# Casting weight transfers, fp32 sums, a spare accumulator bank and a rank table in an attention-and-mixer kernel

## The chip, the cores and the metric

The kernel runs on one core of a Trainium2 chip. The metric is the device time of one execution in microseconds (us); lower is better. The kernel before takes 185.1 us (median of 3 runs, 184.88 to 185.16). Each profiled run also has a span (first to last recorded instruction) and a granted TensorE clock, 1.0 being full speed; within one run the span is about 1.75 us shorter than the time (185.26 and 183.5 in the profiled run before). A "half clock" is 0.5.

## The reference

Four batches, each an attention part (a gated recurrence, 8 heads of 48) and a mixer with two pairs of products. Cut to what matters:

```python
# attention, per batch and head; q, k, v, f_logit: (4, 8, 768, 48) fp32
f = 1 / (1 + exp(-f_logit))
for t in range(768):
    state = f[t][:, None] * state + outer(k[t], v[t])
    y[t] = q[t] @ state
# mixer, per batch; x: (768, 384), the heads side by side
h  = relu(x.T @ w_tok1) @ w_tok2        # w_tok1 768x256, w_tok2 256x768
u  = x + h.T
out = u + relu(u @ w_ch1) @ w_ch2       # w_ch1 384x1536, w_ch2 1536x384
```

The kernel does the recurrence in chunks of 128 steps, two at a time (a "pair"; three pairs a batch). It needs running sums of log f within a chunk, the exponentials of their positive and negative, gated q and k, scores under a mask, and a state that is carried on.

## The kernel before

The kernel describes its work as 972 operations (960 after the change), each with the engines that may do it, an estimated duration and a priority. A planner in the file simulates the engines and emits the instructions in the order that it finds. So a change of a duration, a priority or a part moves instructions everywhere. `patience` is 0 in this kernel. The parts that matter here:

```python
# which ready operation goes next: earliest start, then priority
key = (round(st + self.patience * max(o.prio, -20.0), 2), o.prio, st + occ)
...
# running sums: Ln = ln(1 + exp(-f)); two rows are added (Pf), split into
# a bf16 high part and the bf16 rest, and summed by two bf16 matmuls
P.op(f"hi{i}", {"POOL": ..., "ACT": ...}, [f"Pf{i}"], [f"hi{i}"], ...)    # cast
P.op(f"lo{i}", flex, [f"hi{i}", f"Pf{i}"], [f"L{i}"], ...)                # Pf - hi
nc.tensor.matmul(s3, lhsT=tri2, rhs=hi[:, :, 0:D], start=True, stop=False)
nc.tensor.matmul(s3, lhsT=tri2, rhs=lo[:, :, 0:D], start=False, stop=False)
...
# token weights: fp32 loads after the last v of batch 0, then casts
P.op("w1l", {"SP": (0.7, 0)}, [], ["w1s"], <load>, -400, [tail])
P.op(f"w1c{j},{kk}", {"POOL": ..., "ACT": ...}, ["w1s"], [f"w1{kk}"], <cast>)
# first channel weights: casting DMAs that start after a gate
gates = dict(zip(("wc1a", "wc1b", "wc2a", "wc2b"), ("w2s1", "-", "q1,1", "-")))
...
# products that nobody uses, in TensorE's planned gaps, to keep its clock up
FILL = (1.6, 60.0)        # us of the plan in which they may stand
```

"First token product" below is x times w_tok1, "second token product" is times w_tok2, "channel products" are times w_ch1 and w_ch2, "unused products" are those of the last lines.

## Time and profile before

The profile's own lines are in the prediction further down. This is what they come to; "channel stretch" is from the start of the first channel product to the end of the last, the "ramp" is what comes before it and the "tail" what comes after. A matmul's recorded time overlaps that of the next one (326 ns each, 162.5 ns apart), so a TensorE that reads as busy can still lose time.

| before | us | where it is read |
|---|---|---|
| time, span | 185.1, 183.5 | runs, page |
| end of batch 0's first token product | 35.1 | chain of waits |
| first channel product | 41.0 | chain of waits |
| channel stretch | 137.9 | chain of waits |
| last addition and stores | 4.6 | chain of waits |
| TensorE idle in the channel stretch | 3.4 | windows, below |

In a row of windows the columns are: the stretch, its length, then busy time (and count) of PE (TensorE), PEld (its weight loads), DVE (VectorE), ACT (ScalarE) and POOL (GpSimd), then the clock, the DMA share and GB/s.

### The profile page before, as it was taken

What the parts mean: (1) busy time and instruction counts of PE and PEld (TensorE: products, weight loads), DVE (VectorE), ACT (ScalarE), POOL (GpSimd) and SP (SyncE); (2) the same over time, 40 slices, a digit from 0 to 9 for tenths busy, and PEclk for the clock granted to TensorE, in tenths of its full rate; (3) what the DMA queues carried; (4) which work ended last, traced back from release to release, by engine and by line L of the source; (5) the groups of instructions that cost most, each with busy time, mean ns of one, the idle gap of its engine ahead of it and who ended that gap; (6) DMA issues with size and microseconds to landing.
All of it is one profiled execution on the core that took longest, in us unless ns stands there. A gap on an engine that the chain in (4) does not pass through costs nothing.

```text
span 183.5 us, 5042 instructions
## 1 busy us (share of the span) xinstructions
PE 170.7 (93%) x2050; PEld 105.9 (58%) x2050; DVE 121.7 (66%) x232; ACT 119.6 (65%) x215; POOL 67.9 (37%) x114
## 2 busy tenths in 40 slices
PE   6899979999999999999989999789999999999990
PEld 2346655576666766565656666266666656666550
DVE  7489865698857688998499996998944166012021
ACT  2879689999767688767777935369338542924800
POOL 3017882365374337386543935365210100000000
PEclk9999997999999999999999999999999999999999
DMA  6999999989993999999999999991352011303033
GB/s 151 261 261 263 298 326 241 209 206 257 203 209 85 279 257 264 187 187 214 222 268 189 201 274 136 201 240 25 46 84 73 0 45 45 86 0 88 4 91 81
DMA packets 69159, 31.00 MB, mean 169 GB/s; under 512 B 63120, under 2 KB 68496, under 8 KB 69136
## 3 DMA queue, kind: packets, MB, share of 16 engines
q1 hardware_dynamic: 66768, 28.32, 72.7%
q0 software_dynamic: 2368, 2.36, 7.8%
q8 instruction: 16, 0.26, 0.6%
q14 instruction: 7, 0.06, 0.1%
HBM read 25.17 MB, written 4.72 MB: 163 GB/s over the span
## 4 chain that ended last, share of the span: by engine, by line
PE 58%; DVE 15%; DMA 10%; ACT 9%; issue 4%; POOL 1%; DVEq 0%; ACTq 0%; POOLq 0%
PE pp L902 21%; PE pp L927 18%; DMA v_ld<-in_v_dram 8%; DVE qkh L618 3%; DVE xu L861 3%; PE pp L839 2%; ACT G L577 2%; DMA f_ld<-in_f_logit_dram 2%; PE pp L876 2%; DVE AmT L733 2%; PE pp L855 2%; ACT xu L823 2%; PE pp L641 2%; PE pp L798 2%; PE pp L983 2%
## 5 line engine op out<-in xcount | busy, mean ns | idle before, releaser
L927 PE MATMUL pp<-w_ch,zT 128*128 128x384 bf16 x288 | 52.2, 326 | 0.0
L902 PE MATMUL pp<-uT,w_ch 128*128 128x384 bf16 x288 | 51.5, 326 | 0.6 <-DVE zT L911 0.4
L909 ACT ACTIVATE zT<-pp 128x384 bf16<-128x384 f32 x72 | 34.9, 491 | 18.1 <-PE pp L902 17.9
L902 PEld LDWEIGHTS <-w_ch 128*128 128x128 bf16 x288 | 26.9, 98 | 17.2 <-issue 1.0
L927 PEld LDWEIGHTS <-zT 128*128 128x128 bf16 x288 | 27.0, 98 | 16.5 <-issue 0.2
L937 DVE TENSOR_TENSOR xu<-xu,pp 128x384 f32<-128x384 f32 x24 | 13.2, 551 | 29.2 <-PE pp L927 29.0
L983 PE MATMUL pp<-idle 128*128 128x512 bf16 (+4 forms) x82 | 20.7, 339 | 1.5 <-DVE idle L379 1.5
L481 POOL CAST v_bf<-v_ld 64x384 bf16<-64x384 f32 (+1 forms) x28 | 16.2, 577 | 15.8 <-DMA v_ld<-in_v_dram 14.7
L776 DVE TENSOR_TENSOR AmT<-pp,msk 128x1024 bf16<-128x1024 f32 x12 | 14.4, 1219 | 3.0 <-PE pp L769 3.0
L481 POOL CAST x_bf<-xu 128x768 bf16<-128x768 f32 x10 | 8.2, 824 | 20.9 <-ACT xu L823 20.8
L911 DVE TENSOR_SCALAR zT<-pp 128x384 bf16<-128x384 f32 x24 | 12.7, 554 | 4.6 <-PE pp L902 3.7
L733 DVE TENSOR_TENSOR AmT<-pp,msk 128x1024 bf16<-128x1024 f32 x12 | 14.1, 1217 | 2.4 <-PE pp L725 2.3
L607 POOL TENSOR_TENSOR qkh<-q_ld,G 128x384 bf16<-128x384 f32 x14 | 13.0, 940 | 2.4 <-ACT glast L574 2.3
L618 DVE TENSOR_TENSOR qkh<-k_ld,pp 64x384 bf16<-64x384 f32 x24 | 13.2, 550 | 0.5
L983 PEld LDWEIGHTS <-idle 128*128 128x128 bf16 x82 | 7.9, 104 | 8.3 <-issue 2.8
L861 DVE TENSOR_TENSOR xu<-xu,pp 128x384 f32<-128x384 f32 x24 | 11.7, 547 | 0.1
L548 POOL TENSOR_TENSOR Plo<-Pf,Phi 128x384 bf16<-128x384 f32 x10 | 9.1, 914 | 7.0 <-ACT Phi L479 4.5
L536 ACT ACTIVATE f_ld<-f_ld 128x768 f32<-128x768 f32 x12 | 10.1, 838 | 2.5 <-DMA f_ld<-in_f_logit_dram 2.5
L577 ACT ACTIVATE G<-pp 128x768 bf16<-128x768 f32 x12 | 9.7, 811 | 2.8 <-DVE pp L566 2.0
L823 ACT COPY xu<-pp 128x768 f32<-128x768 f32 x11 | 8.8, 797 | 4.1 <-PE pp L786 2.0
L479 ACT CAST u_bf<-xu 128x768 bf16<-128x768 f32 x8 | 6.5, 831 | 6.9 <-DVE xu L861 6.7
L855 PE MATMUL pp<-h1T,w_tok 128*128 128x384 bf16 x48 | 9.9, 325 | 1.3 <-DVE xu L937 1.1
(99 smaller groups left out, 249.4 us busy)
## 6 DMA issues: line engine op xcount, KB each, us to landing
f_ld<-in_f_logit_dram SPq DMA_DIRECT2D x12, 384.0 KB, 5.1
q_ld<-in_q_dram SPq DMA_DIRECT2D x12, 384.0 KB, 6.2
k_ld<-in_k_dram SPq DMA_DIRECT2D x12, 384.0 KB, 6.0
v_ld<-in_v_dram SPq DMA_DIRECT2D x12, 384.0 KB, 6.5
out_dram<-xu SPq DMA_DIRECT2D x22, 192.0 KB, 2.9
w_ch<-in_moe_w_ch_dram POOLq DMA_DIRECT2D x4, 576.0 KB, 9.4
w1s<-in_moe_w_tok_dram SPq DMA_DIRECT2D x1, 768.0 KB, 7.6
v_ld<-in_moe_w_tok_dram SPq DMA_DIRECT2D x1, 384.0 KB, 6.0
```

The source lines that it names most:

```text
L481: (nc.vector if e == "DVE" else nc.gpsimd).tensor_copy(o, x)
L577: P.op(f"G{i}", {"ACT": act_t(768)}, [f"S{i}", f"S1{i}"], [f"G{i}"], lambda: nc.scalar.activation(P[f"G{i}"].rearrange("t j h d -> t j (h ...
L618: nc.vector.tensor_tensor(o, x, g, ALU.mult)
L733: lambda e=e: nc.vector.tensor_tensor(P[f"Am{e}{i}"], P[f"A{e}{i}"].rearrange("p b (a t) -> p (b a) t", t=128), msk2.rearrange("p j t -> p ...
L776: lambda j=j: nc.vector.tensor_tensor(P[f"Am{j}{i}"], P[f"A{j}{i}"].rearrange("p b (a t) -> p (b a) t", t=128), msk[:, j].rearrange("p j t ...
L855: nc.tensor.matmul(pm[:, 0:DM], lhsT=w_tok2[:, kt, tt * 128:(tt + 1) * 128], rhs=P[f"h1{b}"][:, kt, :], start=(kt == 0), stop=(kt == 1))
L861: nc.vector.tensor_tensor(x, x, P[f"up{i}"][:, 0:DM], ALU.add)
L902: nc.tensor.matmul(pm, lhsT=w_ch1[:, kt, cc * 128:(cc + 1) * 128], rhs=uT[:, 3 * th:3 * th + 3, kt, :], start=(kt == 0), stop=(kt == 2))
L909: nc.scalar.activation(P[f"z{i}"], P[f"zp{i}"][:, 0:384], AF.Relu)
L927: nc.tensor.matmul(P[f"op{i}"][:, 0:DM], lhsT=P[f"z{b},{th},{cc}"][:, c0:c0 + 128], rhs=w_ch2[:, cc, :], start=(cc == 0), stop=(cc == NCC ...
L937: nc.vector.tensor_tensor(x, x, P[f"op{i}"][:, 0:DM], ALU.add)
L983: nc.tensor.matmul(P.psum_tile[:, bank, 0:n], lhsT=idle[:, 0:128], rhs=idle[:, 0:n], start=True, stop=True)
```

## The change

Its intent: take casts and subtractions away from the engines that bound the start, let the token weights arrive without an engine's help, and replace the formula for priorities by a table of ranks that was searched for by replaying traces (so the record says; the diff holds only the table). The core of the diff:

```diff
+RANKS = """ 563 564 565 ... 374 """            # one rank per operation, cut
-key = (round(st + self.patience * max(o.prio, -20.0), 2), o.prio, st + occ)
+key = (int(st * 100.0 + 0.5), o.prio, st + occ)
+for o, rank in zip(P.ops, RANKS.split()):
+    o.prio = int(rank)
 # durations corrected, e.g.
-P.op(f"av{i},{e}", {"PE": (0.165, PE_LAT)}, ...
+P.op(f"av{i},{e}", {"PE": (0.205, PE_LAT)}, ...
 # 1. token weights: three casting DMAs from GpSimd, gated on a landed v load
+gates = ... ("w10","w11"), ("w2",), ("wc1a","wc1b","wc2a","wc2b")
+            -> ("v0,1", "-", "-", "q1,0", "-", "q1,2", "-")
 # 2. the bf16 high part read in place
+return P[f"Pf{i}"].bitcast(BF16).rearrange("p h (d two) -> p h d two", two=2)[:, :, :, 1]
 # 3. batch 0, pairs 1 and 2: sums by fp32 matmuls
+nc.tensor.matmul(hd(P[f"S{i}"][:, a, 0:DM]), lhsT=tri2f[:, 0], rhs=x[:, :, 0:D], ...)
 # 4. second token product in two 64-column halves, so that w_tok2 needs no reordering
+w = w_tok2[:, kt, tt * 128:(tt + 1) * 128].rearrange("r (p two) -> r two p", two=2)
+for j in range(2):
+    nc.tensor.matmul(pm[64 * j:64 * j + 64, 0:DM], lhsT=w[:, j], rhs=P[f"h1{b}"][:, kt, :], ...)
 # 5. last output tile in two halves of 192 columns, its two stores on two queues
 # 6. one PSUM bank (accumulator memory) kept free for unused products until 30 us of the plan, before 26
-    P.spare = 26.0
+    P.spare = 30.0
```

## The prediction

> **What bounds the kernel now.** I read the page's busy shares and slices first, then the chain of waits in order of time, then a table by stage, then the groups by shape for what one instruction costs.
>
> ```profile
> span 183.5 us, 5042 instructions
> PE 170.7 (93%) x2050; PEld 105.9 (58%) x2050; DVE 121.7 (66%) x232; ACT 119.6 (65%) x215; POOL 67.9 (37%) x114
> PE   6899979999999999999989999789999999999990
> PEclk9999997999999999999999999999999999999999
> ```
>
> TensorE looks full, but 20.7 us of its 170.7 are products that nobody uses (82 matmuls of the tile `idle` that keep its clock up), and a matmul is counted with its drain, so 93% hides small gaps. So I did not use busy time. I took start-to-start times: 36 matmuls of 384 columns take 5.85 us in the chain, 0.1625 us each, while the group's mean of one is 326 ns.
>
> ```profile
> 14.97 7.02 DMA v_ld<-in_v_dram
> 22.01 0.76 ACT v_bf L479
> 22.77 0.79 ACT xu L823
> ...
> 27.37 0.80 ACT xu L823
> 28.20 0.84 ACT w_tok L479
> 29.17 0.58 PE pp L839 x2
> ...
> 33.08 1.35 PE pp L983 x7
> 34.43 0.65 PE pp L839 x4
> ...
> 41.02 1.08 PE pp L902 x6
> ...
> 104.20 7.53 DMA v_ld<-in_v_dram
> ...
> 118.43 1.94 DVE xu L861 x4
> ...
> 173.05 5.86 PE pp L927 x36
> 178.93 0.55 DVE xu L937
> ```
>
> The reader should see three parts. Until 41.0 us there is a ramp: batch 0's attention waits for loads (the last v load lands at 22.0), then for ScalarE (casts, evictions, and a token-weight cast at 28.2), and only at 41.02 does the first channel matmul (L902) start. From there to 178.9 the chain is mostly TensorE, with one excursion through a v load and VectorE that ends at 123. Then 4.6 us of tail: one addition and the stores.
>
> ```profile
> 23.00:41.00 18.00, 16.13 (x257) 10.96 (x257) 12.53 (x22) 16.41 (x27) 10.01 (x15) 0.91 1.07 244
> 112.00:124.00 12.00, 9.94 (x116) 5.74 (x114) 10.61 (x18) 6.28 (x11) 6.81 (x13) 1.00 1.00 204
> 124.00:179.00 55.00, 54.90 (x465) 33.72 (x463) 22.10 (x40) 28.23 (x56) 5.12 (x8) 1.00 0.22 49
> 30.00:31.00 1.00, 1.00 (x23) 0.94 (x18) 0.23 (x1) 1.00 (x3) 0.00 (x0) 0.50 1.20 232
> ```
>
> The columns are PE, PEld, DVE, ACT, POOL busy, clock, DMA share, GB/s. In the ramp's second half ScalarE is the full engine (16.4 of 18 us). In 112 to 124 VectorE is (10.6 of 12), and TensorE starves. After 124 TensorE is dense and nothing can be won but the tail. At 30 us the clock was granted at half.
>
> **What the Trainium skill says.** (1) "TensorE: Matmul & The Clock Gate", Part 1: an idle window of about 3.4 us halves the clock. The trace agrees in size: the clock falls after the 0.8 us hole in TensorE at 26.2 and stays 0.5 for about 3.4 us (0.71, 0.50, 0.50, 0.58 in the slices from 29 to 33). It also says warm spacing is N/2.4 GHz plus 2.5 ns, 162.5 ns at 384; measured 162.5. (2) "FP8 and Floating Point Precision", TensorE Precision Notes: true FP32 takes four passes. No fp32 matmul runs in the kernel before; the estimate is 4 x 0.1625 = 0.65 us for 384 columns. (3) "DMA: Bandwidth & Descriptors", SWDGE vs HWDGE: a casting transfer must come from GpSimd's software queue; the section on queues adds that engines take the queues in turn. The trace agrees as far as it goes: the four casting transfers of w_ch cost GpSimd 0.86 us each to issue and land after 7.7 to 12.3 us. (4) "TensorEngine Tiling (Array Packing)", Key Properties: changing the tiling mode drains TensorE. Nothing in the trace before isolates that.
>
> **The change part by part.**
> 1. *Token weights by casting DMA.* Removed: casts of w_tok, ScalarE 2 x 0.83 + 0.52 = 2.2 us, GpSimd 2 x 0.83 = 1.7, VectorE 3 x 0.55 = 1.6, all between 24.3 and 31.0, where ScalarE is full. Added: three software DMAs, 3 x 0.86 = 2.6 us of GpSimd, behind one more gate copy (0.19). They start when v of pair 1 has landed (about 16 us) and run beside the last q, k, v loads. The bytes read are the same 1.57 MB, and the DMA engines are at 260 GB/s, so what they take from v of pair 2 is up to 3 us, but the token weights then land beside it and not after it.
> 2. *High half as a view.* The bf16 high part is read in place from the fp32 sum: 12 casts go (ScalarE 8 x 0.51 = 4.1 us, GpSimd 4 x 0.57 = 2.3). In the ramp two of them lie in the chain itself (0.40 and 0.52 at 6.95 and 8.72).
> 3. *fp32 sums in batch 0, pairs 1 and 2.* Removed: two low-part subtractions (0.56 on VectorE, 0.91 on GpSimd) and two S0 subtractions (2 x 0.56). Added on TensorE: 3 fp32 matmuls of 384 columns and 4 tiny ones per pair, 3 x 0.65 + about 0.5 = 2.45 against 0.53 us, so +3.8 us in all, put where TensorE otherwise runs unused products.
> 4. *Second token product in two 64-column halves.* 48 matmuls become 96; if the two halves run side by side the time is the same 7.8 us; the instruction order has five unbroken groups, perhaps 0.2 us of drain each: +1.
> 5. *Last tile in halves, its store on two queues.* The addition falls from 0.55 to about 0.29, and one store issue (0.6) no longer stands behind another: tail 4.6 to 3.8 us.
> 6. *Order and spare bank.* The built orders differ on all engines. Before the first channel matmul the changed TensorE order holds 27,136 columns of unused products, as many as before, but all token products of batch 0 (24 of the second, in one block, against 12) and batch 1's first pair up to its scores.
>
> **The sum.** Counting matmuls in each built order and multiplying by start-to-start times (0.1625 for 384 columns, 0.056 for a transpose, 0.53 for the sums of a pair, 0.025 or less for small ones, 0.42 ns a column for unused products):
> - Before, ahead of the first channel matmul: start 1.5, useful 16.8, unused 11.4, cold clock at the start 2.1: 31.8. Measured 41.0, so 9.2 us of waits and of the clock dip (3.4 x 0.5 = 1.7). After it: useful 126.8 plus 0.2 unused = 127.0 against 178.9 - 41.0 = 137.9: 10.9 lost to waits, mode changes and unequal spacing. Of these 112 to 124 alone has 3.4: its matmuls make 8.6 us in 12.
> - After: ahead 1.5 + 22.0 + 11.4 + 2.1 = 37.0, of which 3.8 are the fp32 sums. The waits there should fall: ScalarE is relieved of 2.2 + 1.0 us in its full stretch, the token product no longer ends behind a weight cast, the clock dip should go, and the fp32 sums fill time in which TensorE had nothing useful. I take a third of 9.2, 3.0: first channel matmul at 40.0, by then with 1.5 us more of the later work done. After it: useful 125.5. For the 10.9 lost I take 7.0: I count 3 to 4 of it as mode changes that stay (with item 4), and suppose that an order chosen by replays removes half of the rest.
> - 40.0 + 125.5 + 7.0 + 3.8 = 176.3 span. The median exceeds the span by 1.6 (185.1 against 183.5), so **177.9, rounded 178 us**. Of the 7.2 us of span, 1.0 comes from the earlier first channel matmul, 1.5 from work moved ahead of it, 3.9 from waits after it, 0.8 from the tail. The two thirds and the half are my choice; no row gives them.
>
> **The rivals.**
> - *The software queue becomes the new wait.* The token and first channel weights land late. For it: transfers of 7.7 to 12.3 us, and the gate of the first channel weights now stands on GpSimd behind a low-part subtraction that needs batch 1's f. I expect issue at about 32, and with 9 us landing at 41, an estimate, just when wanted. Against: the order was tuned with such landings. It would give back 2 to 3 us: 180 to 181.
> - *The DMA is the bound of the ramp anyway.* 4.7 MB of inputs and 1.6 MB of weights at 260 GB/s take 24 us; casts saved on ScalarE then only turn into waits for v. The ramp gains nothing (41 in place of 40, or 43 with the fp32 sums on top), and the rest gives 179 to 181.
> - *VectorE keeps the middle.* At 112 to 124 it is full; the change takes nothing from it there. Only the order can help. If the replays model it badly, the middle's 10.9 stays: 182.
> - *A better one.* The clock dip disappears and the middle becomes dense, 10.9 to 4 lost: 174 to 175.
>
> **Range and chances.** The tail and the dropped casts are near certain, worth some 2 us together; ramp and middle are each uncertain by 2 to 3 us. So 174 to 182 in 8 of 10. Faster by over 2% means under 181.4: 0.82. Within 2%: 0.15. Slower: 0.03, if the software queue blocks GpSimd.
>
> **What would show it.** The first channel matmul near 40 (right) or past 41 (ramp step wrong); no wait of TensorE for w_tok or w_ch; fp32 matmuls of about 0.65 us start to start; the last channel matmul to the end under 4 us; the stretch at the last batch's token products with TensorE over 9/10; no half clock after 10 us. Wrong if v of pair 2 lands past 25, if the token product of batch 0 ends later than 35, or if the time after the first channel matmul exceeds 135.

## More of the kernel before

The channel stretch of the kernel before:

```profile
41.02:178.93 137.91, 134.53 (x1521) 84.09 (x1519) 90.94 (x159) 86.89 (x163) 48.42 (x78) 1.00 0.74 149
```

TensorE is busy in 134.53 of 137.91 us. 2.06 of the 3.38 us that it stands idle lie between 112 and 124, the row that the prediction shows.

## The result

The changed kernel takes 180.55 us (median of 4 runs, 180.53 to 180.85) beside 185.13 us (184.88 to 186.79) of the kernel before. The ratio is 0.974, 95% interval 0.968 to 0.980: faster. Ratios here are the mean time of one kernel's runs over that of the other's of the same rounds, so not quite the ratio of the medians that are quoted. Executions over 1.5% slower than the fastest of the same kernel are left out of the means.

| us | before | predicted | after |
|---|---|---|---|
| time | 185.1 | 178 | 180.55 |
| span | 183.5 | 176.3 | 179.1 |
| first channel product | 41.0 | 40.0 | 42.5 |
| channel stretch | 137.9 | 132.5 | 132.7 |
| last addition and stores | 4.6 | 3.8 | 3.9 |

(The spans are of the profiled runs, which took 185.26 and 180.85 us.) The three stretches account for the gain in span: the first channel product 1.5 us later, the channel stretch 5.2 shorter, the tail 0.6 shorter; together 4.3, or 4.4 unrounded. The gain came entirely after the ramp. The page of the changed kernel:

```profile
span 179.1 us, 5142 instructions
PE 172.4 (96%) x2111; PEld 109.4 (61%) x2111; DVE 113.7 (64%) x221; ACT 112.6 (63%) x201; POOL 70.7 (39%) x123
PE   6999999999999999999999999999999999999991
PEclk9999999999999999999999999999999999999999
```

TensorE has no slice under 9 between the first and the last, and the clock's notch at 30 us is gone. TensorE does more (172.4 us, from 170.7) in a shorter span, and so does GpSimd (70.7, from 67.9); VectorE and ScalarE do less (113.7 from 121.7, 112.6 from 119.6). The same kinds of stretch as shown of before:

```profile
42.62:175.17 132.55, 132.08 (x1482) 84.14 (x1479) 81.50 (x146) 81.26 (x151) 51.91 (x86) 1.00 0.72 149
112.00:124.00 12.00, 11.69 (x165) 7.72 (x164) 10.64 (x22) 8.82 (x18) 7.21 (x16) 1.00 1.09 213
34.00:42.60 8.60, 8.60 (x168) 6.05 (x168) 8.27 (x16) 8.36 (x15) 4.93 (x7) 1.00 1.15 223
```

First row: idle time of TensorE in the channel stretch fell from 3.38 to 0.47 us. Second row: between 112 and 124 VectorE is as full as it was (10.64 of 12 us, from 10.61), yet TensorE now works for 11.69 us (from 9.94) and does 165 matmuls, not 116. The same amount of VectorE work no longer starves it; it is other work that stands there (the rows compare equal times, not equal work). Third row: the end of the ramp. TensorE is "busy" all the time, VectorE and ScalarE nearly so.

The chain of waits of the changed kernel, in order of time (start, length, what):

```profile
29.02 2.02 PE pp L1153 x9
31.04 1.95 PE pp L973 x12
...
34.04 2.15 PE pp L992 x24
...
39.07 0.59 PE pp L1153 x3
...
42.62 0.97 PE pp L1042 x6
...
173.65 1.50 PE pp L1070 x18
175.17 0.35 DVE xu L1080
```

L973 is the first token product, unbroken and ended at 32.99 us (35.08 before). L992 is all of batch 0's second one, L1042 the first channel product. L1153 are unused products: where they stand, the chain says "TensorE" and hides what TensorE would have waited for. That will matter. The last addition takes 0.35 us (0.55 before).

The casting transfers, from issue to landing (KB each, then us):

```profile
w_ch<-in_moe_w_ch_dram POOLq DMA_DIRECT2D x4, 576.0 KB, 9.1
w_tok<-in_moe_w_tok_dram POOLq DMA_DIRECT2D x2, 192.0 KB, 7.2
w_tok<-in_moe_w_tok_dram POOLq DMA_DIRECT2D x1, 384.0 KB, 7.1
```

The token weights were issued at 18.2, 19.2 and 23.5 us and no matmul waited for one. The first half of w_ch1 was issued at 32.8 and landed 8.3 us later, at 41.1, with the first channel product at 42.5.

### The profile page after: what moved, and what is told of

Same layout as the page of the kernel before. It is cut to its first block, busy times and chain, and to the rows that moved or that the text cites.

```text
span 179.1 us, 5142 instructions
## 1 busy us (share of the span) xinstructions
PE 172.4 (96%) x2111; PEld 109.4 (61%) x2111; DVE 113.7 (64%) x221; ACT 112.6 (63%) x201; POOL 70.7 (39%) x123
## 4 chain that ended last, share of the span: by engine, by line
PE 71%; DVE 9%; ACT 6%; DMA 4%; POOL 3%; SPq 2%; issue 2%; DVEq 0%; POOLq 0%
PE pp L1042 20%; PE pp L1090 20%; PE pp L1153 6%; DMA f_ld<-in_f_logit_dram 4%; DVE qkh L752 3%; PE pp L973 3%; PE pp L775 3%; PE pp L992 2%; PE pp L903 2%; PE pp L920 2%; SPq L1109 1%; ACT f_ld L624 1%; DVE AmT L867 1%; PE pp L1016 1%; ACT f_ld L622 1%
## 5 line engine op out<-in xcount | busy, mean ns | idle before, releaser
L1042 PE MATMUL pp<-uT,w_ch 128*128 128x384 bf16 x288 | 51.1, 326 | 0.3 <-ACT uT L497 0.3
L1090 PE MATMUL pp<-w_ch,zT 128*128 128x384 bf16 x276 | 50.3, 326 | 0.0
L1049 ACT ACTIVATE zT<-pp 128x384 bf16<-128x384 f32 x76 | 36.6, 492 | 12.7 <-PE pp L1042 12.7
L1042 PEld LDWEIGHTS <-w_ch 128*128 128x128 bf16 x288 | 27.0, 98 | 17.0 <-issue 0.3
L1090 PEld LDWEIGHTS <-zT 128*128 128x128 bf16 x276 | 25.5, 98 | 16.2 <-issue 0.9
L1153 PE MATMUL pp<-idle 128*128 128x512 bf16 (+7 forms) x75 | 20.1, 361 | 1.5 <-DVE idle L434 1.5
L741 POOL TENSOR_TENSOR qkh<-q_ld,G 128x384 bf16<-128x384 f32 x18 | 16.5, 929 | 5.1 <-PE pp L775 2.3
L1051 DVE TENSOR_SCALAR zT<-pp 128x384 bf16<-128x384 f32 x20 | 10.6, 554 | 3.9 <-PE pp L1042 2.7
L622 ACT ACTIVATE f_ld<-f_ld 128x768 f32<-128x768 f32 x12 | 10.1, 839 | 4.4 <-DMA f_ld<-in_f_logit_dram 4.3
L1001 DVE TENSOR_TENSOR xu<-xu,pp 128x384 f32<-128x384 f32 x24 | 11.8, 549 | 1.0 <-DMA out_dram<-xu 0.5
L700 DVE TENSOR_TENSOR pp<-pp,f_ld 128x384 f32<-128x384 f32 x10 | 5.6, 564 | 9.5 <-PE pp L656 8.2
L1153 PEld LDWEIGHTS <-idle 128*128 128x128 bf16 x75 | 6.8, 104 | 7.8 <-issue 3.4
L642 POOL TENSOR_TENSOR Plo<-Pf 128x384 bf16<-128x384 f32 x9 | 7.4, 825 | 7.3 <-DVE Pf L631 7.1
L624 ACT ACTIVATE f_ld<-f_ld 128x768 f32<-128x768 f32 x12 | 10.2, 846 | 0.2
```

The costliest lines, as they stand in the source:

```text
L622: lambda: nc.scalar.activation(f_(), f_(), AF.Exp, bias=0.0, scale=-1.0), pg - 6)
L624: lambda: nc.scalar.activation(P[f"Lp{i}"].rearrange("t j h dd -> t h j dd")[:, :, :, 0:D] if F32 and b == 0 else f_(), f_(), AF.Ln, bias=1.0,
L741: vec(e).tensor_tensor(o, x, g, ALU.mult)
L1042: nc.tensor.matmul(pm, lhsT=w_ch1[:, kt, cc * 128:(cc + 1) * 128], rhs=uT[:, 3 * th:3 * th + 3, kt, :], start=(kt == 0), stop=(kt == 2))
L1049: nc.scalar.activation(P[f"z{i}"], P[f"zp{i}"][:, 0:384], AF.Relu)
L1090: nc.tensor.matmul(P[f"op{i}"][:, 0:DM], lhsT=P[f"z{b},{th},{cc}"][:, c0:c0 + 128], rhs=w_ch2[:, cc, :], start=(cc == 0), stop=(cc == NCC ...
```

## The experiments

Theory: the time fell because the order leaves TensorE few waits in the channel stretch; the parts matter mainly through what they allow the order. Rival A: the parts by themselves take work off the bounding engines, and the table only trims. Rival B: VectorE's amount of work sets the middle. A further question is the ramp, which went against the prediction. The ranks go with the list of operations, so a part can't be undone under the same table where it changes that list; such runs use the formula's priorities or a table of their own, and say so. Runs that give a wrong result are named.

### The parts without the table

All parts kept, priorities by the old formula.

```diff
 for o, rank in zip(P.ops, RANKS.split()):
-    o.prio = int(rank)
+    pass
```

> All parts of the change, but the order found by the list scheduler from its due times, as in the kernel before, and not from the table of 960 ranks. If the table carries the gain (my theory: the ramp is no shorter with the change, 42.6 us against 41.0 to the first channel matmul, and the gain lies in denser TensorE work after it), the time is 183.5 to 185.5 us and the stretch from the first channel matmul to the last is 136 us or more against 132.5. If the parts carry it (casts gone from ScalarE, the token weights cast by the DMA), the time stays at 180.5 to 182.

187.44 us (187.27 to 187.73), ratio 1.012 (1.007 to 1.017), correct result. First channel product at 44.5, channel stretch 137.3, clock 0.999. The time lies in neither of the two ranges that were expected; the stretch (136 us or more) does as the theory said. With all its parts but no table the kernel is not faster than before: 1.2% slower. The table is worth 6.9 us (187.44 against 180.55), in the spans 2.0 of it in the ramp and 4.6 in the channel stretch. Rival A, that the parts carry the gain and the table only trims, falls (what the parts are worth under equal conditions is seen further down). Its channel stretch:

```profile
44.50:181.80 137.30, 136.03 (x1546) 83.30 (x1535) 85.09 (x151) 83.59 (x152) 49.67 (x85) 1.00 0.70 142
```

Only 1.27 us of it is idle; but it holds 64 matmuls more than with the table (1546 and 1482). It also has more unused products (88, and 75 with the table, counted in the built kernels), which can be a part of the 6.9. Its other losses I did not separate.

### Neither parts nor table

The old parts under the changed durations, with the later spare bank and the halved last tile.

```diff
-    HIV = 1
-    F32P = 2
-    WSW = 1
+    HIV = 0
+    F32P = 0
+    WSW = 0
-COLS = 1
+COLS = 0
-gates = ... ("v0,1", "-", "-", "q1,0", "-", "q1,2", "-")
+gates = ... ("w2s1", "-", "q1,1", "-")
-    o.prio = int(rank)
+    pass
```

> The opposite: none of the parts (hi and lo casts, token weights through fp32 tiles and casts, no fp32 sums, no column halves, the gates of before), no table; left of the change are the scheduler's corrected costs, the later spare bank, and the halved last tile. If corrected costs alone make a better order, 181 to 183 us; my theory says little comes of them without table and parts: 184 to 186, of which the tail takes 0.7.

190.67 us (190.28 to 190.81), ratio 1.029 (1.023 to 1.034), correct, and outside both ranges that were expected. The first channel product comes at 39.3, the channel stretch is 145.7 us, with the clock at half from about 114 to 121 us (0.982 over the run). The changed estimates of durations (with the spare bank) made the old formula's order some 5.5 us worse. That its constants were tuned to the old estimates is a guess that no run tests. Against this run the parts do help under the formula (187.44 from 190.67), but not to where the kernel already was.

### The old parts with a table of their own

As the run before, with ranks that I searched for with some 54,000 trial schedules, scored by the planner's own end.

```diff
-    pass
+    o.prio = int(rank)        # another table of ranks, for the old list of operations
```

> None of the parts (low half by a cast and a difference, sums in bf16, token weights as fp32 loads and engine casts, whole 128-column token products, gates as before, 86 unused products), only the corrected costs, the halved last tile and an order table of its own, found by some 54,000 trial schedules of the planner that start from this kernel's own parts. If the order carries the gain and the parts little: 181 to 183 us, first channel matmul to last 134.5 us or less. If the parts are needed: 184.5 us or more, between that and the 190.7 us of the same parts without a table. What the table was searched against is the planner's own end, not chip replays as the changed kernel's was, so a figure between 183 and 184.5 decides neither.

183.09 us (182.91 to 183.28), ratio 0.991 (0.986 to 0.996), correct; clock 1.0. The first channel product is at 40.0, the channel stretch 137.3, the tail 3.8. So a table alone, without any of the other parts, turned 190.67 into 183.09 (the parts without a table: 187.44), and its ramp is 2.5 us better than the changed kernel's. But its middle kept the hole:

```profile
40.00:177.30 137.30, 134.55 (x1540) 84.91 (x1537) 90.40 (x156) 87.27 (x163) 48.84 (x83) 1.00 0.70 150
110.00:120.00 10.00, 8.19 (x95) 4.84 (x95) 9.48 (x19) 5.61 (x9) 5.63 (x11) 1.00 1.00 246
```

TensorE idles for 2.75 us of the stretch, 1.81 of them here. The chain of waits there:

```profile
112.62 0.57 DVE xu L1100
...
113.20 3.88 DMA out_dram<-xu
117.09 2.40 DVE xu L1001 x5
```

Five additions of u (L1001) were released by a store out of a buffer xu. The time lies in the band that was said to decide neither way; the channel stretch missed the 134.5 us that was to speak for the order alone. What stands: order alone carries a part of the gain. Whether the parts are needed for the rest, or a table scored by replays would find it for the old parts too, stays open.

Four runs with the changed durations, side by side (us; in brackets the first channel product):

| | old parts | new parts | change by the parts |
|---|---|---|---|
| formula | 190.67 (39.3) | 187.44 (44.5) | -3.2 |
| a table of its own | 183.09 (40.0) | 180.55 (42.5) | -2.5 |
| change by a table | -7.6 | -6.9 | |

So the order is worth about 7 us and the parts about 3, each much the same with and without the other. This does not bear out the theory that the parts matter mainly through what they allow the order. The 3.2 may hold some of the clock, which was at half for some 7 us in the run at 190.67, and the two tables were searched in different ways. In both rows the ramp is longer with the new parts.

### One part in the old order

The high half read in place in the kernel before, its 12 casts gone, all else in the same order.

```diff
-P.op(f"hi{i}", ..., lambda e: cast(e, P[f"L{i}"][0][:, :, 0:D], P[f"Pf{i}"][:, :, 0:D]), pg - 4.5)
+P.op(f"hi{i}", ..., lambda e: None, pg - 4.5)
-hi, lo = P[f"L{i}"]
+hi, lo = hi_of(), P[f"L{i}"][1]
```

> One part of the change alone in the kernel before, its order and engine choices kept: the bf16 high half is read in place and the 12 casts are gone. If a part brings little as long as the order was made with it in mind, 184 to 185, all of it in the ramp (two casts of 0.4 and 0.5 us in the chain). Rival, the casts are dear by themselves: 182.5 to 183.5.

185.05 us (183.92 to 185.42), ratio 0.996 (0.991 to 1.001), correct. The first channel product came at 40.3 (0.7 earlier) and the channel stretch took 138.6 (0.7 longer). The casts were in the chain of the ramp, as the prediction said, but the 0.7 us can't be put down to them alone: this profiled run had no clock dip (1.0), that of the kernel before had one (0.989). In all, nothing was gained in the fixed order.

### fp32 sums made cheap

The six large fp32 matmuls and the small ones read the bf16 high halves of the same tiles. The sums are less exact; the result still passed.

```diff
-lhsT=tri2f[:, 0], rhs=x[:, :, 0:D]
+lhsT=hib(tri2f, "p a")[:, 0, :, 1], rhs=hib(x, "p h")[:, :, 0:D, 1]     # high halves
```

> Order, engines and waits of the changed kernel kept, but the fp32 sums of batch 0's pairs 1 and 2 run as bf16 products of the high halves (result less exact on purpose): about 3.5 us of TensorE time less, all before 16 us. If those sums hold up the ramp (the chain names them from 13.6 to 15.9), the first channel matmul moves from 42.6 to about 40.5 and the time is 178 to 179. If the ramp is bound by the loads (last v at 22.0) and then by ScalarE and VectorE, the TensorE only waits: 180.2 to 180.8.

181.81 us (181.48 to 182.24), ratio 0.982 (0.975 to 0.988). Neither expectation came true: it did not gain and it did not stay, it lost 1.3 us. TensorE's rows of this run, then of the changed kernel (PE alone, clock, DMA share, GB/s):

```profile
8.00:10.00 2.00, 0.59 (x3) 1.00 1.28 261
10.00:12.00 2.00, 1.67 (x20) 0.78 1.28 261
12.00:14.00 2.00, 2.00 (x41) 0.50 1.29 261
```

```profile
8.00:10.00 2.00, 2.00 (x6) 1.00 1.29 262
10.00:12.00 2.00, 1.70 (x24) 1.00 1.28 261
12.00:14.00 2.00, 2.00 (x44) 1.00 1.29 261
```

With less to do TensorE is busy for 0.59 us of 8 to 10, and a window at half clock follows. So the fp32 sums stand beside loads, and they do the service of unused products. Their cost is in the chain of the changed kernel; for one of the two pairs of chunks:

```profile
12.51 0.70 PE pp L673 x2
...
13.61 1.49 PE pp L679 x4
15.10 0.79 PE pp L685 x8
```

Each fp32 matmul is two records: one matmul of 384 columns 0.70 us, two more 1.49, the four small ones 0.79; 2.98 us where the prediction had 2.45.

### Second token product in whole columns

128 columns at once, as before; the tokens then land in the wrong rows. Its output is wrong, which doesn't matter for the time.

```diff
-                    if COLS:
+                    if False:
```

> Order and waits of the changed kernel kept, but the second token product in whole 128-column matmuls as before (the result is wrong on purpose, as its columns are then in another order): 48 matmuls in place of 96. The 24 of batch 0 took 2.15 us as halves in the chain, 12 whole ones should take 1.95 and no mode change: 4 x 0.2 to 0.3 = about 1 us less where TensorE is the bound (batches 1 to 3, 0.7 of it): 179.7 to 180.1. If halves cost nothing, 180.5.

180.41 us (180.18 to 180.71), ratio 0.974 (0.969 to 0.979). The channel stretch is 132.2 us, from 132.7. The 48 additional matmuls cost at most half a us in all, not the 1 us of the prediction.

### VectorE's masks halved, in both kernels

Half of each mask multiplication left out, the rest of its tile zeroed at the start; wrong results on purpose.

```diff
-P[f"Am{j}{i}"], P[f"A{j}{i}"].rearrange("p b (a t) -> p (b a) t", t=128),
+P[f"Am{j}{i}"][:, 0:4], P[f"A{j}{i}"].rearrange("p b (a t) -> p (b a) t", t=128)[:, 0:4],
...
+for t in Am_tiles:
+    nc.gpsimd.memset(t, 0.0)
```

> The same edit in the kernel before, its order kept. My theory: the hole of 3.4 us in TensorE at 112 to 124 is VectorE's, so the time falls to 181 to 183 (from 185.1) and the stretch from first to last channel matmul from 137.9 to 134 or 135. Rival, the hole is a late load of v: 184 to 185.

> The changed kernel with every mask multiplication on half its columns (wrong result on purpose; the other half of the tile is zero from the start): VectorE gets back 24 x 0.6 = 14 us of its 114. My theory: in the new order VectorE no longer sets the time after the first channel matmul: 179.4 to 180.4, most of it in the ramp. Rival, VectorE still sets it: 177 to 178.5.

Before: 185.58 us (184.78 to 185.76), ratio 0.999 (0.994 to 1.004); channel stretch 137.3, from 137.9. After: 182.13 us (181.31 to 183.09), ratio 0.981 (0.976 to 0.987); channel stretch 132.5, from 132.7. VectorE has some 9 us less to do (121.7 to 112.7 us, and 113.7 to 104.3), and both stretches stay where they were to 0.6 us. So the amount of VectorE's work over the whole run does not set the stretch, and rival B falls in that form. In the hole itself the edit took little: from 112 to 124 VectorE went from 10.61 to 9.65 us and TensorE's idle time from 2.06 to 1.92. That it is a matter of when VectorE's work stands and not of how much is supported by the changed kernel, which has 10.64 us of it there and no hole, but no run isolates it. The other rival that was named, a late load of v, can be checked in the traces: the chain of the kernel before has such a load (104.20, 7.53 us); the chain of the run with halved masks has none from 95 to 125, and the hole is there. The changed kernel became slower all the same, and the reason lies in my edit. Of this run (VectorE's copy of a mask and GpSimd's new memsets), then of the changed kernel (the same copy):

```profile
2.27 2.77 POOL L473 MEMSET AmT<- 128x1024 bf16 x3
2.62 1.53 DVE L451 COPY tri<-tri 128x128 bf16<-128x128 bf16 x1
```

```profile
2.62 0.13 DVE L450 COPY tri<-tri 128x128 bf16<-128x128 bf16 x1
```

The copy took 1.53 us beside the memsets, 0.13 us without. The Trainium skill, "SBUF — State Buffer", section "Who interferes with whom", says that VectorE in a two-port mode and GpSimd take a shared pair of ports by turns and that the second one waits for the whole instruction; these lines agree that the copy waits (by 1.4 us, which is longer than one memset of 0.92: it ended at 4.15, about where two of the three memsets end, 4.12 as an estimate). VectorE's first sums came about 1.5 us late and the clock was at half from about 9 to 12 us. So this run can't give the time that halved masks would save, only that the channel stretch did not move.

### Fewer unused products

The unused products end at 29, 22 or 10 us of the plan; all else is the same.

```diff
-    FILL = (1.6, 60.0)
+    FILL = (1.6, 29.0)        # or 22.0, or 10.0; in the kernel before: 22.0
```

> The changed kernel with its order and waits, but no unused products where its plan is past 29 us (16 of 75 or so go, those ahead of the token products of batch 0 and between them and the first channel matmul). If they stand in the way of useful work, the first channel matmul comes at 41.5 us or sooner (42.5 before) and the time is 179 to 180. If TensorE only waits there (my theory: ScalarE and VectorE are 97% busy from 34 to 42.6), it stays within 0.4 us of 42.5, and if the clock falls for want of them, the time is 181 to 183.

> The run without unused products past 29 us of the plan came out 1.5 us faster than the changed kernel, with the clock still full: my theory of ScalarE and VectorE alone fell, and the products do stand in the way. Here they stop at 22 us of the plan: 35 are left of 75 (48 with the limit at 29), 4,480 columns or 1.9 us of TensorE time less between 22 and 29. If each of them holds up what comes behind it, another 0.3 to 0.8 us: 178.3 to 178.8. If the stretch to 29 is bound by the loads, 179.1 as with the limit at 29. If the clock falls for want of them, 180 or more and a granted clock of 0.99 or less.

> The unused products stop at 10 us of the plan: only the 14 at the start are left. This should find the point at which they are needed: useful work fills perhaps half of TensorE between 10 and 22 us, so the clock falls for one window of 3.4 us or more: 180 to 183 and a granted clock of 0.98 or less. If the clock holds nonetheless, 178 to 178.8.

> The same limit of 22 us in the kernel before (50 unused products of 82 left). If the products held up its ramp too, as they do in the changed kernel, 183 to 184.5 and the first channel matmul at 40.3 or sooner. If the clock falls longer than before (it fell for 3.4 us with them), 185.5 to 187.

| run | unused products | time (us) | ratio (95%) | first channel product | clock, profiled run |
|---|---|---|---|---|---|
| changed kernel | 75 | 180.55 | 0.974 (0.968 to 0.980) | 42.5 | 1.0 |
| until 29 | 48 | 179.09 | 0.965 (0.962 to 0.968) | 41.5 | 1.0 |
| until 22 | 35 | 181.03 | 0.975 (0.970 to 0.980) | 43.2 | 0.977 |
| until 10 | 14 | 182.56 | 0.986 (0.982 to 0.990) | 44.8 | 0.952 |
| before, until 22 | 50 of 82 | 185.12 | 1.000 (0.996 to 1.004) | 41.2 | 0.975 |

All four results are correct. In the kernel before, the same limit gained nothing (neither of the two expectations came true). In the changed kernel ending them at 29 gives the best kernel: 178.77 to 179.34 us, 1.5 us under the changed kernel. My count of what would go was wrong (27 products, 9,216 columns, not 16). The channel stretch is 132.1 to 132.2 us in all three runs with fewer (132.7 in the changed kernel), so they differ from each other in the ramp alone, and the best of them from the changed kernel by 1.0 us in the ramp and 0.5 after it. Two things pull against each other there. Too many stand in the way of useful matmuls: the 27 removed are 3.9 us of TensorE (9,216 columns at 0.42 ns), and the first channel product came 1.0 us sooner. Too few, and the clock falls. TensorE's rows until 22, then until 29:

```profile
24.00:26.00 2.00, 1.55 (x66) 1.00 1.22 295
26.00:28.00 2.00, 1.42 (x56) 0.88 1.24 239
28.00:30.00 2.00, 1.33 (x28) 0.50 1.16 287
30.00:32.00 2.00, 1.26 (x5) 0.50 0.80 187
```

```profile
24.00:26.00 2.00, 1.75 (x69) 1.00 1.23 285
26.00:28.00 2.00, 1.67 (x70) 1.00 1.24 244
28.00:30.00 2.00, 1.72 (x36) 1.00 1.14 271
30.00:32.00 2.00, 1.62 (x10) 1.00 0.96 225
```

Busy for 1.4 to 1.55 of 2 us the clock went to half; busy for 1.62 or more it stayed. This is no threshold: in the kernel before TensorE was busy for 0.92 of 2 us from 116 to 118, and the clock stayed at 1.0. The run until 22 is on the edge: its six times fall in two groups, 179.0 and 179.5 us at a clock of 0.996 and 1.0, and 181.0 to 182.0 at 0.971 to 0.977.

Without the unused products the chain of waits shows what they had covered. The run until 29, between the first token product and the first channel product:

```profile
31.42 1.31 PE pp L973 x7
...
32.76 0.87 ACT h1T L978 x2
33.63 0.60 ACT f_ld L624
...
34.27 0.81 ACT G L711
35.09 0.08 ACT glast L708
...
35.19 0.80 ACT pp L713
35.98 1.47 ACT u_bf L497 x2
37.45 0.70 ACT uT L497
38.15 0.92 ACT qkT L497
...
41.59 1.08 PE pp L1042 x6
```

ScalarE works without a pause from 32.76 to 39.07. It evicts the token product (h1T), then does 2.3 us for the exponentials and logarithms of batch 1 (f_ld, G, glast, pp), then the casts and evictions that the channel product needs (u_bf, uT). In the changed kernel's chain the same stretch reads as TensorE. The order put batch 1's work ahead of batch 0's channel product, on ScalarE too. That this holds the ramp is read from the chain; no run moved these exponentials behind the casts.

## Why the prediction was right, and where it was not

The total was right: 180.55 us lies in the range, and the direction was given 0.82. The largest term of its sum, 3.9 us less waiting after the first channel product by a better order, is what the runs bear out: the table alone makes the channel stretch 4.6 us shorter (137.3 to 132.7). By its steps:

- **Time after the first channel product.** Predicted 125.5 useful and 7.0 lost, 132.5; measured 132.7, so 7.2 lost. The split of the loss was off: I took 3 to 4 us as mode changes and half of the rest as gone. Idle time fell from 3.4 to 0.5, nearly all of it, while what is lost between busy matmuls went from 7.5 (10.9 less 3.4) to 6.7. So that 7.0 fits so closely is partly luck: the prediction itself says that no row gives its fractions. The column halves, which I put into that, cost at most 0.5 us.
- **Tail.** Predicted 3.8, measured 3.9: an addition of 0.35 (I said 0.29). To the span the prediction added 1.6 us, a median less the span of another run; in the profiled runs the difference is 1.75.
- **The ramp: the step that failed.** "I take a third of 9.2, 3.0: first channel matmul at 40.0". It came at 42.5, past the 41 that the prediction named as the sign of a wrong ramp step, and this 2.5 us is nearly the whole error of the span (179.1 against 176.3). Above the sum's 37.0 stand 5.5 us, not 3.0. Two terms of the 37.0 were off: the fp32 sums took 2.98 us for the pair in the chain and not 2.45, and the 11.4 us of unused products are not all a floor, for 1.0 us of the ramp goes with those after 29 (shown by the run). The rest is read from the chain: ScalarE does 2.3 us for batch 1 between the token product and the casts. The relief that I credited was there up to the token product, which ended at 33.0 and not 35.1; after it stands batch 1's work, put ahead. The sum has TensorE's share of that work (1.5 us), but not ScalarE's.
- **A contradiction in the working.** The first rival has w_ch1 landing at 41 "just when wanted", while the sum has the product at 40.0. It landed at 41.1, so 40.0 was not to be had. The rival itself did not come true: no matmul waited for a software-queue transfer. But in the run until 29 it landed at 40.7 (issued at 33.1, 7.6 us), 0.8 us ahead of use; a gain of more than that in the ramp needs an earlier gate.
- **The other rivals.** DMA as the bound of the ramp: v of the last pair landed at 22.0 as before, so the token weights beside it did not delay it. "VectorE keeps the middle, only the order can help": VectorE stayed as full there, and the order did help. The halved masks show only that its total work is not the limit.
- **The clock.** Predicted: no half clock after 10 us. True of the changed kernel's profiled run; its three others had 0.996 or 0.997, and where is not recorded. The prediction sets the page's idle window of 3.4 us beside the trace and says that they agree; what lasted 3.4 us was the half clock. TensorE was busy for 2.21 of the 3.41 us before it, so this was no idle window. In the kernel before a dip costs 1.7 us (3.4 at half speed), and on the chip it ran in 183.96 to 186.5 us as the clock of a run was 0.998 or 0.975. So about 1 us of the 4.6 is the clock, an estimate from 185.13 less 183.96.
- **fp32 sums.** 0.65 us a matmul predicted, 0.70 to 0.75 measured; and what I priced as a cost keeps the clock up: without it the clock fell.
- **The credits by part** (2.2 us of token-weight casts, 4.1 of high-half casts) gave a good picture of ScalarE's load (119.6 to 112.6 us), but not of time: all the parts together are worth 2.5 to 3.2 us under equal conditions, and the one that was tested alone in the kernel before (the high half) brought nothing clear of noise.

Open: whether the parts are needed for the last 2.5 us (183.09 with old parts and a table of their own, 180.55 with the new), and what the DMAs for the token weights and the spare bank are worth alone.

## What to carry to other kernels

In a kernel whose order is planned, price a change of parts and a change of order apart: here the order was worth about 7 us and all the parts about 3, and changed estimates under the old formula cost 5.5. Unused matmuls that keep the clock up make TensorE look like the bound: to find the wait beneath them, end them earlier and read the chain again, and keep just as many as hold the clock. Before adding up gains, lay each step's time beside the landing of the data that it needs.

## What the Trainium skill lacked or had wrong

- "TensorE: Matmul & The Clock Gate", Part 1: it names an idle window and a busy window of about 3.4 us, and short idle spells between groups of matmuls, but not how busy is busy enough. Here no idle window was needed: TensorE was busy for 1.42 to 1.55 of each 2 us and the clock halved; at 1.62 to 1.75 it stayed. Nor is the busy share alone enough to tell: at 0.92 of 2 us (kernel before, 116 to 118) it stayed too. A run on the edge (ended at 22 us) gave both, 179.0 and 181.3 us.
- "FP8 and Floating Point Precision", TensorE Precision Notes: four passes for FP32 gave an estimate of 0.65 us for 384 columns; the chain shows 0.70 to 0.75. Each such matmul is two records in the trace, which the page does not say.
- "DMA: Bandwidth & Descriptors": its fit for a software-queue transfer (about 2.0 us and the bytes at 436 GB/s) makes, as an estimate, 2.9 us for the first token weights (0.39 MB read each) and 4.7 us for half of w_ch1 (1.18 MB read). Beside other loads they took 7.2, and 8.3 to 10.9 us. The page says that the engines take the queues in turn, but gives no time for a queue beside loads in flight. That these loads are the cause of the difference was not tested.
- "TensorEngine Tiling (Array Packing)", Key Properties: a change of tiling mode drains TensorE. The page has no figure, and 96 half-width matmuls in place of 48 whole ones cost at most half a us here (channel stretch 132.7 against 132.2).
- No page says that products added for the clock hide waits from the chain: the same stretch reads as TensorE with them and as ScalarE without (6.3 us from 32.76 to 39.07).
